# Denominators of all of batch 2's blocks by turning DMAs and GpSimd, longer planned waits for DMAs, and a new table of departures

## The chip, the core and the metric

The kernel runs on one core of a Trainium2 chip. The metric is the device time of one execution in microseconds (us). The engines are called TensorE (PE in the profile, its weight loads PEld), VectorE (DVE), ScalarE (ACT), GpSimd (POOL) and SyncE (SP, which here issues DMAs only). Engines run side by side, each through its own list of instructions, and wait for one another by semaphores.

## The reference

Attention through 32 inducing points for each of 4 batches, then a maxout layer over all 50176 rows (4 x 12544), in float32:

```python
def mab(q, kv):
    s = scale * (q @ kv.transpose(0, 2, 1))
    a = np.exp(s - s.max(-1, keepdims=True))
    a /= a.sum(-1, keepdims=True) + 1e-09
    return a @ kv
h = mab(I, x)              # I: 32 x 128, the same for each batch; x: 4 x 12544 x 128
x = mab(x, h)              # every row of x attends to the 32 rows of h
h1, h2 = x @ w1, x @ w2    # 128 x 1024 each
out = np.maximum(h1, h2) @ w_out
```

max(h1, h2) is h1 + relu(h2 - h1). So the kernel computes relu(e @ (h @ (w2 - w1))) @ w_out plus a linear part e @ (h @ w1 @ w_out), with e the exponentials of the second attention, and divides each output row by its denominator, the sum of that row's 32 exponentials, at the very end.

## The kernel before

A batch's 12544 rows lie as 128 partitions by 98 *chunks*: a chunk is 128 rows. Chunks are gathered into *blocks* of four *quarters*, each quarter up to four chunks wide; the 32 exponentials of a quarter stand in 32 of the 128 partitions, so a block is a tile e2 of 128 partitions by up to 512. There are 28 blocks, seven for each batch: 0 to 6, 7 to 13, 14 to 20 (batch 2; block 20 holds two chunks), 21 to 27 (batch 3).

Per batch the work is:

- `load_x`: seven DMAs from GpSimd's queue, which bring x in and make it float16. Those of the next batch are issued at the end of the last `pool_accum` of a batch.
- `transpose_x_dma` (14 transposing DMAs from SyncE's queue), `pool_scores`, `pool_rest`, `pool_turn` (six transposing DMAs eu to eT) and `pool_accum`: the first attention, done as side work during the blocks of the batch before. Then `small_rep`, `small_h`, `small_hwd` and `small_m1` make the batch's weights.
- `stage` and `stage_exp`: a block's scores on TensorE (in columns, L637) and their exponentials on ScalarE (L656).
- *phases* (`phase`, L1105): four quarters' products e2 x hwd side by side in row groups, into four PSUM banks; each bank is evicted through a relu by ScalarE (L1131) or VectorE (L1134).
- *final products* (`final_one`, L904): relu x w_out, 8 for each chunk, 3136 in all, summed in one PSUM bank for each group of up to four chunks; `linear_last` (L881) adds the linear part of a few groups.
- `evict_group` (L936): VectorE multiplies the group's bank by the reciprocal denominators and SyncE sends it out. The output tiles have six buffers.

The denominators come in two ways:

- `dens` (L698, L708): products of e2 with a matrix of ones on TensorE (one for each chunk column of a block, sometimes for two blocks at once), and a reciprocal on VectorE. Blocks 0 to 20.
- for blocks with `blk.turned`, 21 to 27: `den_turn` (L715), a transposing DMA from SyncE's queue that turns e2; `den_sum` (L725, L727), five additions on GpSimd that sum groups of 32; `den_rp` (L734), a reciprocal on VectorE. The sums lie in two halves of the tile w1T, which even and odd blocks use in turn.

The order of all this is written by a planner. A class `Clock` keeps, for every engine and PSUM bank, the time to which it is planned; the main loop asks again and again whether a phase, a final product, column work or side work is to come next, and writes that instruction. Side work waits in a list `pending` until `ready` says so, by planned times:

```python
if f is den_sum:
    return a[0].den[1] + 7.5 <= now
if f is den_rp:
    return a[0].dsum[1] + 3.0 <= now and a[0].index <= groups[min(state["g"], len(groups) - 1)].blk.index + 1
```

Where the planner expects TensorE to wait, `keep_busy` (L861) writes filler products. A table `DEV` names steps (number of the phase and of final products since) at which the loop is to depart from its rule: 1 holds a phase back, 2 lets it go early, 3 leaves out column work, 4 takes it soon.

Of the kernel before, what the change touches and what calls it, by code (L numbers as in the profile page):

```python
# [16 lines left out]
INF = 1e9  # L17
# [85 lines left out]
def kernel(  # L103
# [17 lines left out]
    P1 = 14  # L121
# [17 lines left out]
    ck = Clock()  # L139
# [49 lines left out]
    w1out = consts.tile([C, C], F16, name="w1out")  # L189
# [7 lines left out]
    with tc.manual_schedule(engines={ET.PE, ET.DVE, ET.Activation, ET.Pool, ET.SP}):  # L197
# [27 lines left out]
        st = [dict() for _ in range(B)]  # L225
# [99 lines left out]
        U = 16  # L325
        NEU = 5
        NU = K // U
# [234 lines left out]
        w_of = {}  # L562
# [43 lines left out]
        blocks = []  # L606
# [8 lines left out]
            assert c0 == K  # L615

        for n, blk in enumerate(blocks):
            blk.turned = n > 20

        def stage(blk, now=True):  # L620
            bi, ps = bank([128, 512])
# [61 lines left out]
        def dens(blk):  # L683

            blks = [blk]
            if 0 < blk.index < len(blocks) - 1:
                nxt = blocks[blk.index + 1]
                if nxt.staged is not None and nxt.staged <= ck.pe and nxt.rp is None and not nxt.turned:
                    blks.append(nxt)
            bi, ps = bank([128, 512])  # L690
            ck.wait(ck.bank[bi], "den bank")
            uid[0] += 1
            rp = rpp.tile([128, 8, 4], F32, name=f"rp_{uid[0]}", tag="rp")
            n = 0
            for blk in blks:
                wd = blk.width
                for t in range(wd):
                    nc.tensor.matmul(  # L698
                        out=ps[:, 4 * (n + t) : 4 * (n + t) + 4],
                        lhsT=blk.e2[:, 128 * t : 128 * (t + 1)],  # L700
                        rhs=ones_q,
                        start=True,
                        stop=True,
                    )
                blk.rp = rp[:, n : n + wd, :]
                n += wd
            end = ck.run(0.029 * n)
            nc.vector.reciprocal(out=rp[:, 0:n, :].rearrange("p t q -> p (t q)"), in_=ps[:, 0 : 4 * n])  # L708
            ck.bank[bi] = ck.on_dve(end, 0.18 + 0.001 * 4 * n)

        def den_turn(blk):
            uid[0] += 1
# [18 lines left out]
        def den_rp(blk):  # L731
            wd = blk.width
            rp = rpp.tile([128, 8, 4], F32, name=f"rpt_{blk.index}", tag="rp")
            nc.vector.reciprocal(out=rp[:, 0:wd, :].rearrange("p t q -> p (t q)"), in_=blk.dsum[0])  # L734
            ck.on_dve(ck.pe, 0.066 + 0.025 * wd)
            blk.rp = rp[:, 0:wd, :]

        def fill(n):
            bi, ps = bank([128, 512])
# [80 lines left out]
        state = {"g": 0, "mm": 0, "lin": 0, "done": 0, "issued": 0, "phase": 0, "since": 0}  # L820
# [52 lines left out]
        def linear_last(end):  # L873

            while held:
                g = held[0]
                if g.full:
                    if st[g.blk.b].get("m1r", INF) > ck.pe:
                        return
                    for s, (q, t) in enumerate(g.chunks):  # L880
                        nc.tensor.matmul(  # L881
                            out=g.ps[:, 128 * s : 128 * (s + 1)],
                            lhsT=g.blk.e2[:, 128 * t : 128 * (t + 1)],
                            rhs=m1bd[:, q, :],
                            start=False,
                            stop=True,
                            skip_group_check=True,
                        )
                    end = ck.run(0.056 * len(g.chunks))
                evict_group(held.pop(0), end)  # L890
# [31 lines left out]
        def evict_group(g, end):  # L922
            n = len(g.chunks)
            while g.blk.rp is None:
                f, a = next(job for job in pending if job[0] in DEN and job[1][0] is g.blk)
# [18 lines left out]
            else:  # L944
                for i, q in enumerate(qs):
# [2 lines left out]
                        g.ps[:, per * i * C : per * (i + 1) * C].rearrange("p (s c) -> p s c", s=per),  # L948
                        g.blk.rp[:, t0 : t0 + per, q : q + 1].broadcast_to((128, per, C)),
                    )  # L950
            ck.bank[g.bank] = ck.on_dve(end, 0.066 + n * 128 / 960.0)
            runs = []
            for s, (q, t) in enumerate(g.chunks):
                qu = g.blk.quarters[q]
# [34 lines left out]
        def want_linear():  # L989
# [12 lines left out]


        DEV = {
# [22 lines left out]
        }  # L1027
        LIMIT = -16

# [142 lines left out]
        def ready(f, a):  # L1172

            now = ck.pe
            if f is den_turn:
                return a[0].staged <= now
# [4 lines that stand above are left out]
            d = st[a[0]]  # L1181
            if f is pool_scores and a[1] >= NEU and ("eT", a[1] - NEU) not in d:
                return False
            if f is pool_turn and a[1] >= NEU and ("sum", a[1] - NEU) not in d:
                return False
            if f is pool_scores:
                return d.get(("T", (U * a[1] + U - 1) // (P1 // 2)), INF) + 8.0 <= now
            if f is pool_rest:
                return d.get(("T", 13), INF) + 6.0 <= now
            if f is pool_turn:  # L1190
                return d.get(("eu", a[1]), (0, INF))[1] <= now
            if f is pool_accum:
                return d.get(("eT", a[1]), (0, INF))[1] + (9.5 if a[0] == 1 else 11.5) <= now and (a[1] < NU - 1 or "et" in d)
            if f is small_rep:
                return d.get("esrr", INF) + 0.3 <= now
            if f is small_h:
                return d.get("haccr", INF) <= now
            if f in (small_hwd, small_m1):
                if f is small_m1 and a[0] == 0 and w_of["w1out"] > now:
                    return False  # L1200
                return d.get("hT4r", INF) <= now
            return True
# [99 lines left out]
        while state["g"] < len(groups) or held:  # L1302
# [1 line left out]
            at_step = (state["phase"], state["since"])  # L1304
            how = DEV.get(10000 * at_step[0] + 100 * at_step[1] + nth, 0)
            side_work()
            if state["phase"] == 3 and "m1" not in st[0] and w_of["w1out"] <= ck.pe and (ck.mode == "full" or final_ready() >= INF):
                small_m1(0)
            if state["phase"] == 4 and blocks[0].rp is None and (ck.mode == "full" or final_ready() >= INF):
                dens(blocks[0])  # L1310
            if held and ck.mode == "full":
                linear_last(0.0)
# [66 lines left out]
```

## Time and profile before

| | |
|---|---|
| median of three runs | 324.33 us (324.07 to 324.45) |
| the profiled execution's own time | 324.04 us |
| its span, first to last instruction | 322.3 us |
| TensorE busy | 315.3 us, 98% |
| VectorE busy | 281.2 us, 87% |
| ScalarE busy | 281.8 us, 87% |
| GpSimd busy | 39.6 us, 12% |
| DMA | 54.12 MB, mean 168 GB/s |
| clock granted to TensorE | 1.0 throughout |

In the profile, times count from the span's first instruction. A row of the timeline gives start, busy time, engine, line, operation, tiles (out<-in) and how many instructions are merged; idle time before it stands in brackets with what ended it. Matrix products overlap one another, so a busy TensorE is not TensorE at its peak. DMAs of SyncE's queue go by q1, those of GpSimd's by q0; "to landing" is from a DMA's issue to its completion.

### The profile page before, as it was taken

To read this page: it belongs to the slowest core of one execution; us is meant where nothing else is said; L and a number is where in the kernel's file an instruction comes from. 1 tells how busy PE (TensorE), PEld (TensorE's weight loads), DVE (VectorE), ACT (ScalarE), POOL (GpSimd) and SP (SyncE) were. 2 spreads that over 40 slices of the span, in tenths; PEclk is the share of its full clock that TensorE was granted. 3 is DMA by queue.
4 is the path that set the end of the run, shared out by engine and by line. 5 is a ranking of instruction groups with operands and counts; after the bars stand their busy time and mean duration, and the time that the engine had idled before them with its cause. 6 is when DMAs were issued, how large, how long until landed. Compare 5 with 4: busy or idle time off the path is not lost.

```text
span 322.3 us, 12599 instructions
## 1 busy us (share of the span) xinstructions
PE 315.3 (98%) x5370; PEld 240.0 (74%) x5370; DVE 281.2 (87%) x506; ACT 281.8 (87%) x565; POOL 39.6 (12%) x92
## 2 busy tenths in 40 slices
PE   7899999999999999999999999999999999999996
PEld 4776767777777777776777777777777777777786
DVE  3369999988989998999989989988988999899974
ACT  4789899998978999999898999998869999999960
POOL 7471000000040000000040000000006400302000
DMA  8999999975279999997279999696424322323233
GB/s 208 206 266 213 215 227 189 191 205 138 100 156 243 215 249 200 172 182 182 102 148 242 230 218 196 147 186 178 139 97 102 134 81 101 115 94 122 93 118 116
DMA packets 77464, 54.12 MB, mean 168 GB/s; under 512 B 56128, under 2 KB 65120, under 8 KB 77408
## 3 DMA queue, kind: packets, MB, share of 16 engines
q1 hardware_dynamic: 71232, 39.42, 52.5%
q0 software_dynamic: 6032, 13.83, 21.9%
q8 instruction: 42, 0.69, 1.0%
q14 instruction: 14, 0.11, 0.1%
q10 hardware_dynamic: 144, 0.07, 0.1%
HBM read 27.54 MB, written 25.69 MB: 165 GB/s over the span
## 4 chain that ended last, share of the span: by engine, by line
PE 92%; DMA 5%; ACT 1%; issue 1%; POOL 0%; DVE 0%; POOLq 0%
PE ps L904 62%; PE ps L1105 22%; DMA xn<-in_x_dram 5%; PE ps L637 2%; PE ps L397 2%; PE ps L341 1%; ACT relu L1131 1%; PE ps L698 1%; PE ps L531 0%; PE ps L236 0%; PE ps L315 0%; PE ps L442 0%; PE ps L881 0%; PE ps L266 0%; PE ps L489 0%
## 5 line engine op out<-in xcount | busy, mean ns | idle before, releaser
L1131 ACT ACTIVATE relu<-ps 128x512 f16<-128x512 f32 x462 | 244.1, 605 | 23.1 <-PE ps L1105 15.0
L1134 DVE TENSOR_SCALAR relu<-ps 128x512 f16<-128x512 f32 x322 | 206.3, 682 | 16.6 <-PE ps L1105 15.1
L904 PE MATMUL ps<-woutp,relu 128*128 128x128 f16 x3136 | 216.9, 220 | 0.0
L904 PEld LDWEIGHTS <-relu 128*128 128x128 f16 x3136 | 176.6, 98 | 39.4 <-issue 29.0
L1105 PE MATMUL ps<-e,hwd 32*128 32x512 f16 (+2 forms) x888 | 88.2, 358 | 0.6 <-ACT hwd L504 0.6
L936 DVE TENSOR_TENSOR o<-ps,rp 128x512 f32<-128x512 f32 (+3 forms) x80 | 51.2, 640 | 1.8 <-PE ps L904 1.1
L1105 PEld LDWEIGHTS <-hwd 32*128 32x128 f16 x888 | 24.6, 91 | 22.0 <-issue 0.9
L1105 PE MATMUL ps<-m,e 32*128 32x128 f16 x381 | 38.7, 217 | 0.0
L1105 PEld LDWEIGHTS <-e 32*128 32x128 f16 x381 | 21.2, 92 | 2.9 <-issue 0.4
L936 DVE TENSOR_TENSOR o<-ps,rpt 128x512 f32<-128x512 f32 (+3 forms) x28 | 17.3, 618 | 4.1 <-PE ps L881 2.2
L166 POOL DMA_DIRECT2D xn<-in_x_dram x33 | 18.2, 564 | 6.0 <-DMA xn<-in_x_dram 3.8
L164 POOL COPY pace<-hacc 128x1 f32<-128x1 f32 x2 | 0.4, 183 | 129.0 <-DVE hacc L430 129.0
L247 DVE COPY xT<-ps 128x768 f16<-128x768 f16 (+6 forms) x11 | 4.7, 459 | 8.8 <-PE ps L236 8.8
L558 POOL COPY m1bd<-m 32x128 f16<-32x128 f16 x5 | 1.4, 285 | 78.9 <-DVE m L553 76.6
L352 ACT ACTIVATE eu<-ps 128x512 f16<-128x512 f32 x18 | 10.9, 616 | 0.1
L656 ACT ACTIVATE e<-ps 128x512 f16<-128x512 f32 (+2 forms) x21 | 10.4, 570 | 0.2 <-PE ps L637 0.2
L236 PE MATMUL ps<-identity,xn 128*128 128x128 f16 x98 | 8.7, 231 | 1.6 <-DMA xn<-in_x_dram 0.9
L725 POOL TENSOR_TENSOR w1T<-den 128x256 f32<-128x256 f16 (+1 forms) x7 | 4.4, 631 | 38.7 <-DMA den<-e 38.7
L250 ACT COPY xT<-ps 128x768 f16<-128x768 f16 (+5 forms) x10 | 6.5, 671 | 2.7 <-PE ps L236 2.6
L727 POOL TENSOR_TENSOR w1T<-w1T 128x64 f32<-128x64 f32 (+4 forms) x28 | 8.4, 300 | 2.2
L236 PEld LDWEIGHTS <-xn 128*128 128x128 f16 x98 | 6.3, 103 | 3.0 <-DMA xn<-in_x_dram 1.9
L637 PE MATMUL ps<-xT,hT 128*32 128x512 f16 (+3 forms) x118 | 8.4, 355 | 0.0
(94 smaller groups left out, 116.0 us busy)
## 6 DMA issues: line engine op xcount, KB each, us to landing
out_dram<-o SPq DMA_DIRECT2D x68, 256.0 KB, 2.6
xn<-in_x_dram POOLq DMA_DIRECT2D x24, 448.0 KB, 10.0
out_dram<-o SPq DMA_DIRECT2D x54, 128.0 KB, 1.8
wf<-in_moe_w_dram POOLq DMA_DIRECT2D x4, 256.0 KB, 6.0
xn<-in_x_dram POOLq DMA_DIRECT2D x3, 224.0 KB, 8.7
xT<-xn SPq DMA_TRANSPOSE x42, 4.2
xf<-in_x_dram SPq DMA_DIRECT2D x1, 512.0 KB, 3.5
xf<-in_x_dram SPq DMA_DIRECT2D x1, 384.0 KB, 4.0
```

The costliest lines, as they stand in the source:

```text
L166: nc.gpsimd.dma_start(out=xn_at[b, i][lo:hi, 0:n, :], in_=xr[b, lo:hi, k0 : k0 + n, :])
L236: nc.tensor.transpose(ps[:, j, :], xn_at[0, i][:, g + j, :], identity16)
L250: nc.scalar.copy(out=dst, in_=ps[:, 0:m, :])
L352: nc.scalar.activation(out=eu, in_=ps, func=AF.Exp, scale=scale, accum_out=st[b]["es"][:, u : u + 1])
L637: nc.tensor.matmul(out=ps[32 * q : 32 * (q + 1), 128 * t : 128 * (t + n)], lhsT=hq, rhs=xT[:, c : c + n, :], start=True, stop=True, tile_p ...
L656: nc.scalar.activation(out=blk.e2[:, lo:hi], in_=ps[:, lo:hi], func=AF.Exp, scale=st[0]["rs"] if blk.b == 0 else scale,)
L727: nc.gpsimd.tensor_add(acc[:, :, 0:n], acc[:, :, 0:n], acc[:, :, n : 2 * n])
L904: nc.tensor.matmul(out=g.ps[:, 128 * c : 128 * (c + 1)], lhsT=g.blk.relu[q][:, 128 * (jb * w4 + t) : 128 * (jb * w4 + t + 1)], rhs=woutp[: ...
L936: nc.vector.tensor_mul(osb[:, 0:n, :], g.ps[:, 0 : n * C].rearrange("p (s c) -> p s c", s=n), rp)
L1105: nc.tensor.matmul(**seq[i])
L1131: nc.scalar.activation(out=dst, in_=src, func=AF.Relu)
L1134: nc.vector.tensor_scalar(out=dst, in0=src, scalar1=0.0, scalar2=None, op0=ALU.max)
```

## The change

Four things change:

- `blk.turned` holds for blocks 14 to 27, so batch 2's blocks leave `dens` as well.
- The planner counts the time at which a block's reciprocals are ready (`rpr`) when it plans the eviction of a group, and 0.45 us more for the product m1 that `linear_last` needs.
- Scores of the first attention are planned 9.0 us after their transposing DMA in place of 8.0; accumulations of batches 2 and 3 are planned 12.3 us after their turn in place of 11.5. The first product m1 and the first denominators may come in later phases than the third and fourth.
- The table `DEV` has 31 entries in place of some 150. With that the planner writes another order from the third phase on.

`den_turn`, `den_sum`, `den_rp` and the rules of `ready` for them are as before. The instructions in the new order: 25 products of L698 fewer, 3 reciprocals of L708 fewer and 7 of L734 more, 7 transposing DMAs on SyncE's queue and 35 additions on GpSimd more, two fillers more.

```diff
         for n, blk in enumerate(blocks):
-            blk.turned = n > 20
+            blk.turned = n > 13
...
             ck.bank[bi] = ck.on_dve(end, 0.18 + 0.001 * 4 * n)
+            for blk in blks:
+                blk.rpr = ck.dve + 0.2
...
             blk.rp = rp[:, 0:wd, :]
+            blk.rpr = ck.dve + 0.2
...
-                    if st[g.blk.b].get("m1r", INF) > ck.pe:
+                    if st[g.blk.b].get("m1r", INF) + 0.45 > ck.pe:
                         return
...
-            ck.bank[g.bank] = ck.on_dve(end, 0.066 + n * 128 / 960.0)
+            ck.bank[g.bank] = ck.on_dve(max(end, g.blk.rpr), 0.066 + n * 128 / 960.0)
...
         DEV = {
-            50900: 2, 61200: 2, 81400: 1, 100300: 1, 110700: 1, 110900: 1, 111100: 1, 111500: 1, 111600: 1,
...
-            1370100: 3, 1370900: 1, 1380100: 1, 1391300: 1, 1410000: 2, 1420300: 2, 1421400: 1
+            20000: 2, 50900: 2, 61200: 2, 111700: 1, 151400: 1, 160800: 1, 201400: 1, 210000: 3, 220000: 3,
+            221200: 2, 230000: 3, 240000: 3, 271000: 2, 281200: 2, 301200: 2, 331400: 1, 331500: 1, 370000:
+            3, 481300: 1, 661400: 1, 760000: 3, 841400: 1, 1031400: 1, 1311200: 2, 1360000: 3, 1411300: 1,
+            1421300: 1, 1501300: 1, 1521300: 1, 1591100: 2, 1651300: 2
         }
...
-                return d.get(("T", (U * a[1] + U - 1) // (P1 // 2)), INF) + 8.0 <= now
+                return d.get(("T", (U * a[1] + U - 1) // (P1 // 2)), INF) + 9.0 <= now
...
-                return d.get(("eT", a[1]), (0, INF))[1] + (9.5 if a[0] == 1 else 11.5) <= now and (a[1] < NU - 1 or "et" in d)
+                return d.get(("eT", a[1]), (0, INF))[1] + (9.5 if a[0] == 1 else 12.3) <= now and (a[1] < NU - 1 or "et" in d)
...
-            if state["phase"] == 3 and "m1" not in st[0] and w_of["w1out"] <= ck.pe and (ck.mode == "full" or final_ready() >= INF):
+            if state["phase"] >= 3 and "m1" not in st[0] and w_of["w1out"] <= ck.pe and (ck.mode == "full" or final_ready() >= INF):
                 small_m1(0)
-            if state["phase"] == 4 and blocks[0].rp is None and (ck.mode == "full" or final_ready() >= INF):
+            if state["phase"] >= 4 and blocks[0].rp is None and (ck.mode == "full" or final_ready() >= INF):
                 dens(blocks[0])
```

20 rows, old and new, of the table DEV are left out of this document.

## The prediction

> **What bounds the kernel now.** I read the page first, then the timeline around the places that the change touches, then the DMA view of single stretches. From the page, the span, the busy times and the chain by engine:
>
> ```profile
> span 322.3 us, 12599 instructions
> PE 315.3 (98%) x5370; PEld 240.0 (74%) x5370; DVE 281.2 (87%) x506; ACT 281.8 (87%) x565; POOL 39.6 (12%) x92
> PE 92%; DMA 5%; ACT 1%; issue 1%; POOL 0%; DVE 0%; POOLq 0%
> ```
>
> TensorE is busy for 98% of the span and is 92% of the chain that ended last. So one instruction less on TensorE is time gained, and any stretch in which TensorE stands is time lost: nothing later gives it back. VectorE and ScalarE have 13% to spare, on the average. The profiled execution took 324.04 us, 1.74 more than its span; the median of the three runs is 324.33, 0.29 above it. The sum below is made against 324.04. A difference of 0.2% (0.65 us) is about the least that can be told from none.
>
> The timeline, ordinary rounds (start, busy us; "PEld" rows are weight loads and show when TensorE's queue moves on):
>
> ```profile
> 149.95 0.10 PEld L904 LDWEIGHTS <-relu 128*128 128x128 f16 x1
> 150.15 0.10 PEld L1105 LDWEIGHTS <-hwd 32*128 32x128 f16 x4
> ...
> 152.22 0.30 PEld L698 LDWEIGHTS <-e 128*128 128x128 f16 x8
> 152.45 0.23 PEld L904 LDWEIGHTS <-relu 128*128 128x128 f16 x4
> ...
> 178.16 0.10 PEld L1105 LDWEIGHTS <-hwd 32*128 32x128 f16 x4
> 178.49 0.79 PEld L904 LDWEIGHTS <-relu 128*128 128x128 f16 x14 [0.23 <-issue]
> 179.38 0.10 PEld L1105 LDWEIGHTS <-hwd 32*128 32x128 f16 x4
> ```
>
> A phase (L1105) and 14 final products take 179.38 - 178.16 = 1.22 us, a final product (L904) about 0.06. Going from finals to a phase takes 0.20 (149.95 to 150.15), where a further final would have taken 0.06.
>
> **The change, part by part.** What stands where in the changed kernel I take from the recorded order of its instructions; the prices are rows.
>
> *Products removed.* Blocks 14 to 20 lose 25 denominator products (L698, 76 become 51). Eight of them took 152.45 - 152.22 = 0.23 us, so 25 take 0.72: **-0.7 us**, all on TensorE. The kinds and numbers of all other products stay (222 runs of phases in both), but for two fillers more, priced below.
>
> *Column work entered from finals.* It is entered 26 times in both orders, from finals 7 times before and 5 after, otherwise from a phase, which has to be left anyway. Two turns of 0.20 - 0.06: **-0.3 us**.
>
> *The start.* Before, TensorE waits for GpSimd's copy of m1:
>
> ```profile
> 25.94 0.37 PEld L861 LDWEIGHTS <-warm 128*128 128x128 f16 x4
> 26.52 0.30 PEld L1105 LDWEIGHTS <-hwd 32*128 32x128 f16 x7 [0.21 <-issue]
> ...
> 27.28 0.10 PEld L881 LDWEIGHTS <-e 128*128 128x128 f16 x1
> 27.88 0.22 PE L881 MATMUL ps<-m1bd,e 128*128 128x128 f16 x1 [0.43 <-POOL m1bd L558]
> 28.02 0.09 PEld L1105 LDWEIGHTS <-hwd 32*128 32x128 f16 x1 [0.65 <-issue]
> ```
>
> From L881's load to the next phase are 0.74 us, of which 0.20 are the turn: 0.54 lost. The new order puts this phase ahead of the product of L881, and six fillers in place of four (0.1 each by the first two rows). -0.54 + 0.2 = **-0.3 us**; bounds -0.6 (the shorter waits before 27 go too) and +0.3 (the phase finds no free banks earlier).
>
> *The new table and the longer planned waits* change order alone. The planner writes fillers where it foresees a wait of some tenths, and both orders have them only in the first phases: it foresees no long wait. I put this at 0, with 0 to +1.5 in the range.
>
> *Denominators by DMA and GpSimd.* Before, blocks 21 to 24 go this way. SyncE's turning DMAs, GpSimd's sums and VectorE's reciprocals of these blocks:
>
> ```profile
> 242.13 2.50 SPq L715 DMA_TRANSPOSE den<-e  x2
> 245.35 3.67 SPq L715 DMA_TRANSPOSE den<-e  x2
> ...
> 244.69 0.66 POOL L725 TENSOR_TENSOR w1T<-den 128x256 f32<-128x256 f16 x1 [0.79 <-DMA den<-e]
> 245.43 1.46 POOL L727 TENSOR_TENSOR w1T<-w1T 128x128 f32<-128x128 f32 x4
> 246.84 0.67 POOL L725 TENSOR_TENSOR w1T<-den 128x256 f32<-128x256 f16 x1
> ...
> 253.48 0.24 DVE L734 RECIPROCAL rpt<-w1T 128x16 f32<-128x16 f32 x1
> ```
>
> A turn takes SyncE 1.25 us; a block's sums take GpSimd 246.84 - 244.69 = 2.15; the first reciprocal ran 253.48 - 242.13 = 11.35 us after the first turn. The seven new sums (15 us of GpSimd) and the seven reciprocals (1.7 us of VectorE, less three that go) lie beside TensorE's work, as long as VectorE does not wait. VectorE's queue is in order: behind a reciprocal that waits stand the relu evictions that free TensorE's banks.
>
> This is where the change can lose. In the new order the turns of blocks 14 to 17 follow their scores at once; the four sums stand in one row; the reciprocals of 14 and 15 stand in VectorE's queue right after the output whose last final is about the 1580th. The four blocks share two halves of w1T: the reciprocal of 14 waits until the sums of 16 are through, that of 15 for those of 17. So four sums have to be done by the time VectorE gets there.
>
> *When VectorE gets there.* Before, at that place:
>
> ```profile
> 163.92 0.38 PE L531 MATMUL ps<-w,hT 128*128 128x512 f16 x1
> 165.39 1.60 ACT L656 ACTIVATE e<-ps 128x512 f16<-128x512 f32 x3
> 179.83 0.68 DVE L936 TENSOR_TENSOR o<-ps,rp 128x512 f32<-128x512 f32 x1
> ```
>
> In the new order the same output stands some 3 finals later (+0.2), after one phase less (-0.4), one stage of scores more (+0.2) and the gains above (-0.7 or so): the reciprocal is reached at about 179.6. The weights of batch 2 (L531) stand 20 finals later (+1.2) less 0.7, at about 164.4; the four exponentials (0.53 each) follow as before 1.5 later, the first done at 166.4. SyncE then turns 14 at 166.4, 15 at 167.7, 16 at 168.9, and 17 after one output at about 170. From 166.4 to 179.6 are 13.2 us; 11.35 were enough above.
>
> *But the DMA engines are not those of 242 us.* The DMA view of 162 to 176.9 us (issues by tile, KB, median us to landing), of 166 to 182 (packets of the queues), of 241 to 250, and of 102.35 to 112.3, with the two transposes that were issued while batch 2 was loading:
>
> ```profile
> q0 software_dynamic: 686, 2.23, 79.8%
> xn<-in_x_dram POOLq DMA_DIRECT2D x7, 448.0 KB, 12.5
> out_dram<-o SPq DMA_DIRECT2D x5, 256.0 KB, 8.4
> ```
> ```profile
> q0 software_dynamic: 841, 2.67, 84.4%
> q1 hardware_dynamic: 724, 1.12, 21.9%
> ```
> ```profile
> DMA packets 2465, 1.07 MB, mean 118 GB/s; under 512 B 2208, under 2 KB 2208, under 8 KB 2464
> den<-e SPq DMA_TRANSPOSE x4, 3.0
> ```
> ```profile
> xT<-xn SPq DMA_TRANSPOSE x2, 10.7
> ```
>
> Batch 3's seven loads of x are issued at 162 to 166, just ahead of the turns, in both orders. While they run, an output takes 8.4 us to land, and a transpose 10.7, where the turns of 242 took 3.0. SyncE's queue q1 gets 724 / 16 = 45 packets a us then, about as many as the loads' q0. A turn has 2208 / 4 = 552 small packets: 552 / 45 = 12.2 us for the first alone. That q1 gets no more when its packets are small is seen at 109.4 to 110.2, when the transposes of batch 2 came up beside the loads:
>
> ```profile
> DMA packets 82, 0.18 MB, mean 225 GB/s; under 512 B 29, under 2 KB 29, under 8 KB 82
> q0 software_dynamic: 43, 0.15, 95.7%
> q1 hardware_dynamic: 39, 0.03, 14.4%
> ```
>
> 29 small packets among 39, against 43 of the loads: still one for one. [...]
>
> So: the output ahead of block 14's turn, issued at about 165, lands 8.4 later, 173.4. From there 45 packets a us. The loads (7 x 448 KB = 3.2 MB; 2.23 moved by 176.9, then 2.67 / 16 = 0.17 a us) end at about 182.5; by then 410 of the 552 packets are through, and the rest goes fast. Turn 14 lands at about **184** (182 to 188). The other turns follow quicker than GpSimd sums. Sums of 16 done: 184 + 3 x 2.15 = 190.5; of 17: 192.6. VectorE stands from 179.6 to 192.6, **13 us**. Behind the two reciprocals stand two relu evictions of the next two phases; TensorE goes on for some 40 finals, until a phase at about the 1623rd final needs their banks, and then stands as well. SyncE stands at the next output. How much TensorE's wait is shorter than VectorE's is VectorE's slack:
>
> ```profile
> 162.00:188.00 26.00, 26.00 (x422) 19.77 (x417) 24.19 (x43) 24.35 (x47) 3.69 (x7) 1.00 1.05 208
> ```
>
> 24.19 of 26 us busy (third engine column): 1.8 us free, so about 1 us of 13 is caught up. **+12 us** on TensorE.
>
> The turns of 18 to 20 (at about 203 us, no loads then) need three turns on SyncE, 3 us of landing and under 6.5 of sums, some 10 to 11 us; their reciprocal stands four outputs, about 12 us, later: 0, and 2 us if SyncE is late.
>
> **Sum.** 324.04 - 0.7 - 0.3 - 0.3 + 12 = **334.8 us**.
>
> **The rivals.**
>
> 1. *VectorE waits for the turned sums behind the loads* (above): 334.8, by the bounds of the landing (182 to 188) and of the slack 331 to 339.5. Chance 0.66.
> 2. *The turns are no slower than outputs.* Then 14 lands at 166.4 + 8.4 = 174.8, 17 is summed 8.6 later at 183.4, VectorE stands for 3.8, TensorE for about 2.8: 325.5. [...] For it: the packets of 109.4 to 110.2 are few. Against it: the 10.7 us of the transposes. Chance 0.16.
> 3. *The cover holds*, on the other side: the turns land within 4.6 us, the sums are through by 179.6, and what is left is the gain on TensorE: 324.04 - 1.3 = 322.7. It decides at a landing of 179.6 - 8.6 - 166.4 = 4.6 us. For it: 3.0 us at 242, and the 11.35 us that were enough. Against it: no issue of that queue in the rows of the loads' stretch has a median below 8.4. Chance 0.13.
> 4. *The change does not keep its gain*: short waits of the new order eat 1 us of it and the turns cost nothing: 323.7. Chance 0.05.
>
> **How the numbers follow.** The likeliest case gives 334.8. Cases 1 and 2 hold 0.82; the range takes both, from 325 to 339.5, and leaves out 3 and 4. Faster by over 0.2%: case 3, 0.13. Within 0.2%: case 4, 0.05. Slower: 0.82.
>
> **What would show it.** Right: in the profile after, the landing of the first four turns takes over 10 us, VectorE's first reciprocal of a turned block waits for GpSimd for some 10 us near 180, TensorE has one gap as long shortly after, and the rest of the span is as before less 1.3 us. Wrong: turns that land in under 5 us near 167, or gaps of TensorE elsewhere, at batch 3's scores or accumulations. Case 2 shows as a gap of 2 to 4 us there.

## The result and the profile after

| | before | after |
|---|---|---|
| median | 324.18 us (324.07 to 324.45, 5 runs) | 338.92 us (336.95 to 339.27, 5 runs) |
| the profiled execution | 324.04 us | 338.92 us |
| its span | 322.3 us | 337.1 us |
| mean clock granted to TensorE | 1.000 | 0.979 |

The ratio is 1.0439, with a 95% interval from 1.0408 to 1.047: the changed kernel is 14.7 us slower. In the listing after, every line number above 620 or so is shifted: L717 is the turning DMA, L727 and L729 the sums, L736 the reciprocal, L1090 a phase, L907 a final product, L1119 VectorE's relu, L939 an output (sent by SyncE at L967).

The page of after, from its parts on busy time, slices and the chain:

```profile
span 337.1 us, 12623 instructions
PE 318.4 (94%) x5347; PEld 241.7 (72%) x5347; DVE 280.8 (83%) x510; ACT 281.7 (84%) x565; POOL 51.8 (15%) x127
...
PE   7899999999999999999996099999999999999996
...
PEclk9999999999999999999999569999999999999999
...
PE 85%; DMA 10%; POOL 2%; ACT 1%; issue 1%; DVE 0%; POOLq 0%
PE ps L907 56%; PE ps L1090 21%; DMA den<-e 5%; DMA xn<-in_x_dram 4%; PE ps L637 2%; PE ps L341 1%; PE ps L397 1%; POOL w1T L729 1%; ACT relu L1116 1%; POOL w1T L727 1%; PE ps L531 0%; PE ps L698 0%; PE ps L236 0%; PE ps L315 0%; PE ps L442 0%
```

One slice of 40 has TensorE at 0, with a 6 ahead of it: a single hole, which the timelines below put at 182 to 194 us. The chain that ended last now leads through the turned denominators (DMA den<-e 5%, which is 17 us, then POOL w1T). The clock row has a 5 and a 6 at the hole and the slice after it: besides the hole, TensorE worked at half clock there.

The timelines of SyncE, GpSimd, VectorE and TensorE's weight loads around the hole:

```profile
163.45 2.72 SPq L967 DMA_DIRECT2D out_dram<-o  x2
167.13 13.43 SPq L717 DMA_TRANSPOSE den<-e  x3
180.65 0.56 SPq L967 DMA_DIRECT2D out_dram<-o  x1
181.30 1.25 SPq L717 DMA_TRANSPOSE den<-e  x1
...
163.92 3.99 POOL L166 DMA_DIRECT2D xn<-in_x_dram  x7 [0.77 <-PE ps L442]
183.39 0.66 POOL L727 TENSOR_TENSOR w1T<-den 128x256 f32<-128x256 f16 x1 [15.48 <-DMA den<-e]
186.69 0.67 POOL L727 TENSOR_TENSOR w1T<-den 128x256 f32<-128x256 f16 x1 [1.10 <-DMA den<-e]
191.78 1.48 POOL L729 TENSOR_TENSOR w1T<-w1T 128x128 f32<-128x128 f32 x4
...
180.07 0.68 DVE L939 TENSOR_TENSOR o<-ps,rp 128x512 f32<-128x512 f32 x1
191.12 0.25 DVE L736 RECIPROCAL rpt<-w1T 128x16 f32<-128x16 f32 x1 [10.37 <-POOL w1T L729]
193.29 0.25 DVE L736 RECIPROCAL rpt<-w1T 128x16 f32<-128x16 f32 x1 [1.92 <-POOL w1T L729]
193.47 1.22 DVE L1119 TENSOR_SCALAR relu<-ps 128x512 f16<-128x512 f32 x2
...
182.17 0.10 PEld L1090 LDWEIGHTS <-hwd 32*128 32x128 f16 x3
194.15 0.10 PEld L1090 LDWEIGHTS <-hwd 32*128 32x128 f16 x1 [11.88 <-issue]
194.68 1.30 PEld L907 LDWEIGHTS <-relu 128*128 128x128 f16 x13 [0.44 <-issue]
```

Read from the top, this is one chain. GpSimd issues batch 3's seven loads from 163.92; SyncE issues the turn of block 14 at 167.13. GpSimd can begin to sum it only at 183.39, so turn 14 took 16.2 us to land. The four sums end at 193.26. VectorE stands 10.37 us at the reciprocal of block 14 (for the sums of 16) and 1.92 us at that of block 15 (for those of 17), and only then comes to the relus that free the banks. TensorE stands 11.88 us at the fourth row group of a phase (L1090). The last row shows a second thing: 13 finals now take 1.30 us, 0.1 each, where 14 took 0.79 before.

The DMA view of 168 to 180 us (packets, MB and share of each queue; then issues, count, median us to landing):

```profile
q0 software_dynamic: 660, 2.08, 92.1%
q1 hardware_dynamic: 539, 0.36, 14.5%
den<-e SPq DMA_TRANSPOSE x3, 16.8
```

While the loads run, SyncE's queue (q1) gets 539 packets in 12 us, 45 a us, against 55 of the loads (q0). The table by stretch (length; busy us and instructions of PE, PEld, DVE, ACT, POOL; granted clock; DMA share; GB/s):

```profile
160.00:182.00 22.00, 22.00 (x382) 16.97 (x380) 18.42 (x37) 19.43 (x37) 3.90 (x8) 1.00 0.87 171
182.20:194.10 11.90, 0.36 (x3) 0.07 (x3) 1.06 (x4) 0.99 (x2) 7.52 (x20) 0.66 0.99 212
194.10:199.70 5.60, 5.55 (x48) 4.08 (x48) 4.45 (x7) 2.51 (x5) 0.00 (x0) 0.50 0.39 103
199.70:337.00 137.30, 134.02 (x2250) 103.71 (x2247) 120.81 (x214) 117.13 (x233) 18.72 (x54) 1.00 0.46 124
```

The hole is 11.9 us, and the 5.6 us behind it run at a granted clock of 0.50. The stretches ahead of it and behind it run at 1.00.

### The profile page after: what moved, and what is told of

It reads as the page before. It is cut to its first block, busy times and chain, and to the rows that moved or that the text cites. A ratio compares the mean times of both kernels' runs of the same rounds, so it can differ in the third digit from the quotient of the medians.

```text
span 337.1 us, 12623 instructions
## 1 busy us (share of the span) xinstructions
PE 318.4 (94%) x5347; PEld 241.7 (72%) x5347; DVE 280.8 (83%) x510; ACT 281.7 (84%) x565; POOL 51.8 (15%) x127
## 4 chain that ended last, share of the span: by engine, by line
PE 85%; DMA 10%; POOL 2%; ACT 1%; issue 1%; DVE 0%; POOLq 0%
PE ps L907 56%; PE ps L1090 21%; DMA den<-e 5%; DMA xn<-in_x_dram 4%; PE ps L637 2%; PE ps L341 1%; PE ps L397 1%; POOL w1T L729 1%; ACT relu L1116 1%; POOL w1T L727 1%; PE ps L531 0%; PE ps L698 0%; PE ps L236 0%; PE ps L315 0%; PE ps L442 0%
## 5 line engine op out<-in xcount | busy, mean ns | idle before, releaser
L1119 DVE TENSOR_SCALAR relu<-ps 128x512 f16<-128x512 f32 x322 | 205.8, 681 | 18.2 <-PE ps L1090 16.9
L907 PE MATMUL ps<-woutp,relu 128*128 128x128 f16 x3136 | 217.9, 221 | 0.1
L907 PEld LDWEIGHTS <-relu 128*128 128x128 f16 x3136 | 178.2, 98 | 39.8 <-issue 29.5
L1090 PE MATMUL ps<-e,hwd 32*128 32x512 f16 (+2 forms) x888 | 90.2, 360 | 12.2 <-DVE relu L1119 11.6
L1090 PEld LDWEIGHTS <-hwd 32*128 32x128 f16 x888 | 25.1, 91 | 34.2 <-issue 13.4
L1090 PE MATMUL ps<-m,e 32*128 32x128 f16 x381 | 39.1, 218 | 0.0
L939 DVE TENSOR_TENSOR o<-ps,rpt 128x512 f32<-128x512 f32 (+3 forms) x54 | 34.3, 634 | 5.1 <-PE ps L907 3.1
L939 DVE TENSOR_TENSOR o<-ps,rp 128x512 f32<-128x512 f32 (+3 forms) x54 | 34.2, 633 | 0.9 <-PE ps L907 0.6
L1090 PEld LDWEIGHTS <-e 32*128 32x128 f16 x381 | 21.3, 93 | 2.6
L727 POOL TENSOR_TENSOR w1T<-den 128x256 f32<-128x256 f16 (+2 forms) x14 | 8.7, 624 | 71.1 <-DMA den<-e 47.2
L729 POOL TENSOR_TENSOR w1T<-w1T 128x32 f32<-128x32 f32 (+5 forms) x56 | 16.8, 300 | 4.4
L736 DVE RECIPROCAL rpt<-w1T 128x16 f32<-128x16 f32 (+2 forms) x14 | 3.3, 236 | 12.3 <-POOL w1T L729 12.3
```

The source lines that it names most:

```text
L727: nc.gpsimd.tensor_add(acc, eT[:, :, 0 : M // 2], eT[:, :, M // 2 : M])
L729: nc.gpsimd.tensor_add(acc[:, :, 0:n], acc[:, :, 0:n], acc[:, :, n : 2 * n])
L907: nc.tensor.matmul(out=g.ps[:, 128 * c : 128 * (c + 1)], lhsT=g.blk.relu[q][:, 128 * (jb * w4 + t) : 128 * (jb * w4 + t + 1)], rhs=woutp[: ...
L939: nc.vector.tensor_mul(osb[:, 0:n, :], g.ps[:, 0 : n * C].rearrange("p (s c) -> p s c", s=n), rp)
L1090: nc.tensor.matmul(**seq[i])
L1119: nc.vector.tensor_scalar(out=dst, in0=src, scalar1=0.0, scalar2=None, op0=ALU.max)
```

## The experiments

Theory A is the prediction's: turns 14 to 17 run beside batch 3's loads of x, land late, and VectorE's reciprocals hold TensorE up. The runs were made in two groups on other chips; the kernel before took 324.25 us (324.14 to 324.78) beside the first group (the loads after the turns, the reciprocals' own sums, the 105 fillers, the turn from block 18 on) and 324.27 us (324.18 to 324.34) beside the other four. The planner writes the order anew for every edit, so a run with another `blk.turned` differs from its base in more than the turns.

### Loads after the turns

```diff
-            if last and b + 1 < B:        # in pool_accum
+            if last and b + 1 < B - 1:
...                                        # in den_sum
+            if blk.index == 14:
+                for i in range(7):
+                    load_x(3, i)
+                st[3]["loads"] = True
...                                        # batch 3's transposes come later
-            t_first, t_step = (6, 2.2) if b == 1 else (-6, 3.4)
+            t_first, t_step = (6, 2.2) if b == 1 else (-6, 3.4) if b == 2 else (4, 2.8)
```

> The changed kernel, but batch 3's seven loads of x are issued from GpSimd's queue behind block 14's sums, in place of ahead of them; batch 3's transposes follow some 8 us later. Theory A (the turns of blocks 14 to 17 share the DMA engines packet by packet with the loads): the first turn lands within 4 us in place of 16.2, the four sums are through before VectorE gets to the reciprocals, VectorE waits under 1 us there, TensorE's gap of 11.9 us and the half clock behind it go: 338.9 - 14.5 = about 324.4 us, +-1. Theory B (GpSimd's four sums in a row are what takes long, the landing matters little): VectorE still waits over 5 us, 330 us or more. Theory C (the new table and planned waits cost the time): no change, 338.

Measured: 335.0 us (334.54 to 335.94), ratio 1.0333 (1.0314 to 1.0351). First the DMA view of 167 to 170 us and that of 172.4 to 178 us, where the loads run (from 172.53 on):

```profile
den<-e SPq DMA_TRANSPOSE x2, 2.4
```
```profile
den<-e SPq DMA_TRANSPOSE x1, 5.9
```

Then its timeline, of VectorE and TensorE (here L740 is the reciprocal and L1094 a phase; L341 makes the scores of the first attention):

```profile
181.03 0.24 DVE L740 RECIPROCAL rpt<-w1T 128x16 f32<-128x16 f32 x1
183.03 0.25 DVE L740 RECIPROCAL rpt<-w1T 128x16 f32<-128x16 f32 x1 [1.75 <-POOL w1T L729]
183.88 0.09 PEld L1094 LDWEIGHTS <-hwd 32*128 32x128 f16 x1 [1.26 <-issue]
...
221.60 0.39 PE L341 MATMUL ps<-xT,inducingT 128*32 128x512 f16 x2 [0.86 <-DMA xT<-xn]
224.25 0.38 PE L341 MATMUL ps<-xT,inducingT 128*32 128x512 f16 x1 [2.26 <-DMA xT<-xn]
```

Without the loads the first turns land in 2.4 us in place of 16.2; the one that the loads overtake takes 5.9. The reciprocal of block 14 does not wait, and the hole of 11.88 us is 1.26, with a granted clock of 1.00 behind it. That settles the cause of the hole: it is the loads beside the turns. The total was missed by 10 us: with the loads 8.6 us later, the scores of batch 3's first attention (L341) wait for the transposes of x, four times and 5.0 us in all, and behind these waits the granted clock is 0.50 twice, from 207.58 to 210.99 and from 224.64 to 228.06. Final product by final product, the run is 1.3 us behind the kernel before at the 1623rd final, 5.4 at the 1901st and 11.1 at the 2101st. So moved by 8.6 us, the loads do not solve it: what the hole cost is paid again some 20 us later.

### Each reciprocal waits for its own sums only

```diff
-                return a[0].den[1] + 7.5 <= now        # ready, den_sum
+                two = blocks[a[0].index - 2]
+                return a[0].den[1] + 7.5 <= now and not (two.turned and two.rp is None)
```

Sums of block 16 are written after the reciprocal of 14, so that the two halves of w1T no longer make 14 wait for 16.

> The changed kernel, but a block's sums are planned only after the reciprocal of the block two before it, so that the reciprocals of 14 and 15 wait for their own sums alone (in the changed kernel that of 14 waits for the sums of 16, that of 15 for those of 17). Theory A: the turns land as before (183 to 188 us), VectorE goes on after the sums of 15 at about 189.0 in place of 193.5: TensorE's gap is 4.4 us shorter, 338.9 - 4.4 = 334.5 us, with the half clock behind a gap of some 7.5 us still there or a little shorter. If only the landing counts: 338.9.

Measured: 333.1 us (332.74 to 335.09), ratio 1.0283 (1.0252 to 1.0314). Its timeline:

```profile
185.76 0.25 DVE L736 RECIPROCAL rpt<-w1T 128x16 f32<-128x16 f32 x1 [5.00 <-POOL w1T L729]
189.02 0.25 DVE L736 RECIPROCAL rpt<-w1T 128x16 f32<-128x16 f32 x1 [3.01 <-POOL w1T L729]
189.88 0.10 PEld L1090 LDWEIGHTS <-hwd 32*128 32x128 f16 x1 [7.60 <-issue]
```

The hole is 7.60 us, 4.3 less, which is two blocks' sums of 2.15. So with turns that land late, the shared halves of w1T are a third of the hole; with the early landing of the run above, and the halves shared as in the changed kernel, the hole was 1.26 us. The median fell by 5.8 us, 1.4 more than expected. The profiled execution, the slowest of the four, fell by 3.8 only, so that scatter can make this difference.

### Fillers in the hole

```diff
+        FILL = (120, 105)
...
+            if state["phase"] == FILL[0]:
+                g = groups[state["g"]]
...
+                for _ in range(FILL[1]):
+                    nc.tensor.matmul(
+                        out=g.ps[:, 0:256],
+                        lhsT=warm[:, 0:128],
+                        rhs=warm[:, 0:256],
...
```

The products go into a bank that is open at that time. The tile warm holds zeros, so they add nothing to it and take TensorE's time alone.

> The changed kernel, with 105 filler products of zeros (0.11 us each, 11.5 us) put on TensorE just ahead of the phase at which it stands for 11.9 us. Nothing else is moved. If the half clock between 194 and 200 us comes of TensorE's standing still: the granted clock stays at 1.0, the 5.6 us at half speed become some 2.9, and the time is 338.9 - 2.7 = 336.2 us. If the low clock comes of something else, 338.9 or, if the fillers are slower than 0.11 us, a little more.

Measured: 336.37 us (336.01 to 337.56), ratio 1.0378 (1.0356 to 1.0399), a mean granted clock of 1.000. The stretches:

```profile
182.20:194.10 11.90, 11.90 (x111) 10.30 (x109) 0.85 (x3) 0.63 (x2) 7.50 (x20) 1.00 1.01 217
194.10:199.70 5.60, 5.43 (x83) 4.03 (x81) 5.60 (x11) 4.47 (x9) 0.00 (x0) 1.00 0.51 140
```

The hole is as long, but full, and the clock behind it stays at 1.00: 81 loads of weights in 5.6 us in place of 48. So the half clock here came from TensorE's standing still. Its price is 338.92 - 336.37 = 2.55 us by the medians, which scatter by 2.3 and 1.5 us; by the traces it is 2.1: at the 1660th final, behind the half clock, the changed kernel is 14.46 us behind the kernel before, and this run 12.36.

### Half the fillers

The same with 60 fillers in place of 105.

> The changed kernel with 60 filler products in place of 105 ahead of the phase that waits: 60 x 0.109 = 6.5 us of the 11.9 are filled, TensorE then stands for some 5 us, to the same end. If the clock falls about 4 us after TensorE stops, whatever it did before (theory A), it falls at about 193, shortly before the work goes on, and the finals after it run at half clock for some 5 us: 338.5 to 339. If the clock goes by a longer average (rival), 5 us of standing are too few to halve it: 336.4.

Measured: 338.67 us (337.48 to 339.89), ratio 1.0444 (1.0424 to 1.0464). TensorE's weight loads (L1103 is a phase here), and half-us stretches of the clock:

```profile
193.00 0.10 PEld L1103 LDWEIGHTS <-hwd 32*128 32x128 f16 x1 [4.18 <-issue]
193.54 1.30 PEld L907 LDWEIGHTS <-relu 128*128 128x128 f16 x13 [0.44 <-issue]
...
192.00:192.50 0.50, 0.00 (x0) 0.00 (x0) 0.35 (x2) 0.00 (x0) 0.12 (x1) 0.69 0.63 135
198.50:199.00 0.50, 0.50 (x7) 0.43 (x5) 0.00 (x0) 0.50 (x2) 0.00 (x0) 0.50 0.98 369
199.00:199.50 0.50, 0.50 (x10) 0.29 (x9) 0.00 (x0) 0.30 (x1) 0.00 (x0) 0.98 0.25 59
```

TensorE stood for 4.18 us only. The clock fell at about 192.2, under a us before the work went on, and stayed at half until 199.0: the price was as that of the whole hole, and the fillers won nothing (338.67 against 338.92). The first theory of the expectation holds, the longer average does not.

### Turn from block 18 on, in the new order

```diff
-            blk.turned = n > 13
+            blk.turned = n > 17
```

> The changed kernel, with blocks 14 to 17 back on TensorE's denominator products (only 18 to 27 are turned); table and planned waits as changed. Theory A: no gap near 182, clock 1.0; 16 products of 0.03 us come back: 338.9 - 14.5 + 0.5 = 324.9 us, the same as the kernel before within 0.3%. Theory C (table and planned waits): 330 us or more.

Measured: 326.2 us (325.44 to 326.58), ratio 1.0061 (1.0045 to 1.0078). Its hole is gone; at that place TensorE has no more than the ordinary step between a phase and the finals:

```profile
182.03 0.10 PEld L1090 LDWEIGHTS <-hwd 32*128 32x128 f16 x4
182.36 0.73 PEld L907 LDWEIGHTS <-relu 128*128 128x128 f16 x13 [0.23 <-issue]
```

So the turns of 14 to 17, with what the planner moves on their account, are 12.7 us of the change. (It writes four fillers near 245 us, 0.1 us each, that the changed kernel does not have.) What is left, 1.95 us, is more than the 0.65 that were expected; the next two runs take it apart.

### The new order alone, and the turns of 18 to 20 alone

The changed kernel with `n > 20`, and the kernel before with `n > 17`; one line each.

> The changed kernel with turning from block 21 on only, as before: what is left of the change is the new table and the longer planned waits. With turns from block 18 on, this order gave 326.2. If the new order brings its short waits in batch 3's scores by itself (theory A), this gives 325.5 to 326.4 (nine products more, 0.3, and the waits as they were). If they come from the turns of blocks 18 to 20 on SyncE and GpSimd (rival), this gives 324.3 or a little less.

> The kernel before with blocks 18 to 20 turned as well (nine products of the denominators fewer), old table, old planned waits. No loads run when these three turn. Theory A, that turns without loads beside them are hidden: 324.25 - 9 x 0.029 = 324.0, no wait of VectorE for GpSimd. Rival, that three turns of SyncE and 6.5 us of GpSimd delay batch 3's side work: 325 to 326, with waits in batch 3's scores and accumulations at 215 to 245 us.

Measured: the new order alone 325.26 us (325.15 to 325.43), ratio 1.0031 (1.002 to 1.0042); the turns of 18 to 20 alone 325.3 us (324.56 to 328.17), ratio 1.0044 (1.0025 to 1.0064). So each costs about 1 us, and their sum is near the 1.95 of the run before. The new order came out a little under the range of its first theory (325.5 to 326.4) and far from its rival; the turns of 18 to 20 came out as the rival (325 to 326). In the new order alone, against the kernel before, the last final comes 1.28 us later: it is 0.2 behind at the start, 0.0 at the 1801st final, 0.8 at the 1901st and 1.3 at the 2301st, beside batch 3's first attention. That this delay is there without a turn of 18 to 20 shows that the order brings it. The waits that the theory named are not seen: from 200 to 320 us TensorE is busy for 119.91 of 120 us, against 119.40 in the kernel before. Two fillers at 246 us take about 0.2 of it; which steps make the rest is open. For the turns of 18 to 20 the profiled execution (324.89 us) does not show the price: no wait of VectorE for GpSimd, the last final 0.1 later than in the kernel before. Its 12 runs spread over 3.6 us, where 18 of the kernel before lie within 0.16; what makes the longer ones is open.

### All of batch 2 turned, in the old order

The kernel before with `n > 13`; one line.

> The kernel before with blocks 14 to 20 turned as well, and nothing else changed: its own table of departures and its own planned waits stay. If the wait comes from turning beside batch 3's loads (theory A), it comes in this order too: turn 14 lands some 16 us after its issue near 167, VectorE's reciprocal waits for GpSimd for 8 to 11 us near 180, TensorE stands for about 10 us and is at half clock for some 10 us: 324.3 - 0.7 + 10 + 2.5 = 336. If it is the new order that puts the reciprocals too early (rival), the old order has no such gap: 323.5.

Measured: 337.31 us (336.44 to 337.61), ratio 1.0398 (1.0384 to 1.0411). The timeline of VectorE and TensorE:

```profile
191.14 0.37 DVE L734 RECIPROCAL rpt<-w1T 128x16 f32<-128x16 f32 x2 [10.33 <-POOL w1T L727]
192.10 0.10 PEld L1105 LDWEIGHTS <-hwd 32*128 32x128 f16 x1 [9.78 <-issue]
192.64 1.30 PEld L904 LDWEIGHTS <-relu 128*128 128x128 f16 x13 [0.44 <-issue]
```

The old order has the same hole at the same place, 9.78 us, with half clock behind it. Only three sums stand ahead of the reciprocals there, so it is some 2 us shorter. The 1.3 us above the 336 expected are about what the turns of 18 to 20 cost in this order (1.0). Turning batch 2's first blocks is what costs the most, not the table. (L734, L727, L1105 and L904 are the reciprocal, the sums, a phase and a final product, as in the kernel before.)

## Why the prediction was right, step by step

The forecast was 334.8 us (325 to 339.5); it came out at 338.92, slower by the mechanism named.

- *Turn 14 lands at about 184 (182 to 188).* Issued at 167.13 and not 166.4, summed from 183.39. The mechanism held: a packet of the turns for a packet of the loads (524 each from 173 to 182 us). The rate was taken too low, 45 a us in place of the 58 that stand below this list; with 58 the prediction's own sum gives 173.4 + 552 / 58 = 182.9, so little hung on it. The second case, a landing at 174.8, did not come.
- *The other turns follow quicker than GpSimd sums.* Nearly: GpSimd waited 1.10 us for the second. Unforeseen was SyncE: the third turn's issue held it until 180.56, so that turn 17 went out at 181.30 in place of 170. It landed before GpSimd came to it. So three of the first four turns took over 10 us to land (16.2 to 18.1), and the fourth 6.8.
- *Sums of 16 done at 190.5, of 17 at 192.6; VectorE stands from 179.6 for 13 us.* 191.1 and 193.26; from 180.75, for 10.37 + 1.92 = 12.3 us. Of these, 0.4 us were caught up where the prediction had 1.
- *TensorE stands for 12 us, at about the 1623rd final.* 11.88 us; at the 1623rd final the run is 12.4 us behind the kernel before, at the 1610th it was 0.35 ahead.
- *Products removed, -0.7.* Borne out as far as it can be seen: at the 1610th final the changed kernel is 0.35 ahead of the kernel before and the new order alone 0.26 behind, so that the 16 products of blocks 14 to 17 are worth some 0.6 us, with a scatter of 0.2 (0.46 by the prediction's price).
- *Blocks 18 to 20 at 0, or 2 if SyncE is late.* Turned in the kernel before they cost 1.0 us, with the gain of their nine products already in it: inside the bounds, not at the value taken.
- *The new table at 0, with 0 to 1.5.* The new order alone, which holds it together with the start and the column work, is +1.0 where the sum had -0.6. If those two gains came, the table cost 1.6, just outside; if they did not, 1.0.
- *The start, -0.3.* Not there: at the 17th final the changed kernel is 0.13 us behind, the new order alone 0.21. The kernel before with `n > 17`, whose order at the start is the old one, is also 0.23 behind, so about 0.2 is scatter between executions, and the gain of the new order at the start about 0. No run shows the column work's -0.3 by itself.

The rate of SyncE's queue, from the DMA view of 173 to 182 us:

```profile
q0 software_dynamic: 524, 1.65, 95.6%
q1 hardware_dynamic: 524, 0.13, 13.3%
```

524 / 9 = 58 packets a us, one for each of the loads. That 168 to 180 us gave 45, as forecast, is chance: this stretch holds the first us too, in which the queue moved little (8 packets from 168.5 to 170.2). The trace also shows how the pieces take turns: 17 of the loads and 17 of the turns start from 179.40 to 179.60 us, and none in the tenth of a us ahead of it or the one behind it. Over 16 DMA engines that is about one of each on each, an estimate from these counts.

The total was 4.1 us short. The step that was mis-sized is the term for TensorE's wait: the sum took it as 12 us of standing and let the work behind it go on at full speed. 2.1 to 2.55 us more are the half clock, by the run with fillers. The other 1.6 to 2 us are not shown one by one. Candidates are the gains of 0.3 and 0.3, of which the first did not come, the small delays of the new order, and the end: the span is 337.1 - 322.3 = 14.8 us longer, the last final 14.3 us later. The prices of the parts do not simply add: the delay beside batch 3's first attention (1.3 from the 1801st final on in the new order alone) is only about 0.4 behind the hole.

No run here beats the kernel before; the nearest, the new order alone and the turns of 18 to 20 alone, are 1.0 us slower.

## What to carry to other kernels

Work taken off a busy engine and given to DMA was not hidden here beside the loads, where turn 14 took 16.2 us to land in place of the 2.4 of the first turns without them (and even the three turns without loads gained nothing, by the medians): before moving a transfer, look up in the trace what other queue moves large packets in that stretch, and count packets, not bytes: in 9 us the turns' queue got 524 packets as the loads' did, but 0.13 MB against 1.65. Look also at what stands behind the use of the result in its engine's list: here the relus that free TensorE's banks stood behind the reciprocals, and 12.3 us of VectorE's wait became 11.88 of TensorE's. When TensorE is to stand for some us, look up the clock behind the hole as well: behind these 11.88 us it was 0.50 for 5.5 us, which cost 2.1 to 2.55. Filling a part of the hole bought nothing here, as 4.18 us stayed open; a hole of 1.26 us left the clock at 1.00.

## What the runs showed of the hardware

**The half clock came in steps of one length, 3.41 us.** Half-us stretches of the changed kernel:

```profile
185.50:186.00 0.50, 0.00 (x0) 0.00 (x0) 0.00 (x0) 0.00 (x0) 0.09 (x1) 1.00 0.05 4
186.00:186.50 0.50, 0.00 (x0) 0.00 (x0) 0.00 (x0) 0.00 (x0) 0.00 (x0) 0.53 0.09 12
199.00:199.50 0.50, 0.50 (x8) 0.50 (x7) 0.50 (x1) 0.50 (x2) 0.00 (x0) 0.50 0.06 25
199.50:200.00 0.50, 0.50 (x8) 0.41 (x6) 0.10 (x1) 0.50 (x2) 0.00 (x0) 0.82 1.04 381
```

A mean of 0.53 in a stretch means that the clock fell 0.03 us into it, one of 0.82 that it rose 0.18 us into it: from 186.03 to 199.68, 13.65 us. In the same way the run with 60 fillers had half clock from 192.2 to 199.0, 6.8 us: half as long. The two short stretches of the run with the later loads were 3.41 and 3.42 us, with 13.65 us at full rate between them; the runs with own sums and with all of batch 2 turned in the old order had 10.24 us. So the stretches measured are one, two, three and four steps of 3.41 us. In the changed kernel and the run with 60 fillers the clock fell 3.7 and 3.4 us after TensorE's last load (182.3 and 188.8) and rose 5.5 and 6.0 us after TensorE went on (194.15 and 193.0); in the runs with own sums and with all of batch 2 turned in the old order it rose 6.5 and 4.0 us after (189.88 and 192.10). What sets these times, no run shows. The changed kernel's 5.5 us of work at half speed are an estimate of 2.8 us lost; 2.1 to 2.55 were measured. The executions differ in this too: the fastest of the changed kernel, 336.95 us, has a mean clock of 0.985, which is about 10 us at half rate or three steps (an estimate: 2 x 0.015 x 335.1 us = 10), where the profiled one has four.

**The third turn blocked its queue.** SyncE's row above, "167.13 13.43 ... x3", covers three issues. The second of them by itself, from the same timeline, and the three of the run with the loads moved back, from its timeline:

```profile
168.53 1.68 SPq L717 DMA_TRANSPOSE den<-e  x1
```
```profile
167.48 3.81 SPq L717 DMA_TRANSPOSE den<-e  x3
```

The second was over at 170.21; the third held SyncE from 170.30 to 180.56, 10.26 us. Without loads beside them three issues took 3.81 us together. So here the engine that issues turning DMAs stood for 10.26 us with two earlier ones in flight, and the output behind them, sent at 180.65, stood too.
